# Linear attention beside a small mixture block: the order of the first loads, and two zero products fewer

## The chip, the cores and the metric

The kernel runs on one core of one Trainium2 chip. Five engines work beside each other, each with its own list of instructions: TensorE (PE: matrix products and transposes, with its weight loads listed as PEld), VectorE (DVE), ScalarE (ACT), GpSimd (POOL) and SyncE (SP, which here only issues DMA transfers). ACT and POOL issue some transfers too. PE reads SBUF and writes PSUM, and what it writes must be copied from PSUM to SBUF by another engine before PE can use it again. The metric is the time of one execution in microseconds (us). Times within an execution are counted from the start of its span.

## What is computed

The input x has 2048 tokens of 640 features. All of what follows starts from the layer normalisation xn of x:

```python
xn = _layernorm(x, axis=-1)
return x + A(xn, wqkv, wo) + B(xn, w_r, w_gate, w_up, w_down)
```

Part A is linear attention with 32 heads of 20 features. From q, k, v = xn @ wqkv it forms phi(q) and phi(k), where phi(t) is t+1 for positive t and exp(t) otherwise, with 1e-6 added. It then takes kv = phi(k)^T v and z = the sum of phi(k) over the tokens for each head, and o = phi(q) kv / (phi(q) z), followed by a product with wo.

Part B scores every token by r = xn @ w_r and takes the 8 tokens of highest score. Those go through a gated block (silu(x w_gate) * (x w_up)) w_down, scaled by sigmoid(r), and the result is added to the rows of these tokens. Part B also passes xn itself on, so the output is x + xn + A + the eight rows.

## The kernel before

The tokens are cut into 16 tiles of 128 (t = 0 to 15), the features into 5 chunks of 128 (`KC`). The instructions of each engine stand in the order in which the program text issues them; nothing reorders them. An engine therefore waits at the first instruction whose inputs are not there, and everything behind it on that engine waits too.

**First loads (L108 to L118).** Two queues carry them. SP issues one half of x tile 0, x tiles 1 and 2, chunks 3 and 4 of the k weights (`wk`), chunks 0 and 1 of the q weights (`wq`), x tile 3, and x tiles 4 to 7 in one transfer. ACT issues the other half of x tile 0, chunks 0 to 2 of `wk`, and chunks 2 to 4 of `wq`. The column 640 of `wk` is not loaded with it: it takes the score weights w_r, which come by a small transfer on POOL, are transposed on PE into `prep` (L312), and are copied in by ACT (L313).

**Zero products (`warm_mm`, L273).** PE multiplies a tile of zeros, in products of 512 or 128 columns, whose results nobody reads. Eight long ones come first (L296), then the eight small products of the head mask (`mask_mm`), two more long ones (L298) and two of 128 columns (L305).

**Normalisation.** For each tile, DVE makes two statistics of 320 features (`ln_half`, L165), joins them (`ln_aggr`), and POOL raises the variance to the power one half (L178). For the first four tiles DVE then takes the reciprocal and writes xn (`ln_norm`, L193). Tile 0's xn is written in two pieces, of 256 and of 384 features.

**Transposes.** Tiles 0, 1 and 2 are transposed on PE (`tr_tile`, L202) and copied to `xnT` (`tr_evict`, L208): both copies of tile 0 and the first of tile 1 by ACT, the second of tile 1 by DVE, tile 2's by ACT. From tile 3 on a DMA transpose does it.

**The start of the products.** `k_mm(0)` takes 5 products of 512 columns, one for each chunk, then the transposes of tile 1 stand on PE, then 5 products of 129 columns. `k_mm(1)` and `q_mm(0)` follow, then the transposes of tile 2, then `ga_mm(0)`, which multiplies xn of tile 0 by phi(k) of tile 0 (`pk`). `pk` is made by two ACT passes over k (`ek`, `rk`, L215 and L218) and one DVE pass (L227).

**The loop (L438).** For each t from 2 to 15: k products, `ga_mm` of the tile before, q products on PE, and around them the statistics and normalisation of a tile two or three ahead, phi(k), phi(q), and the later loads. After the loop come the other Gram products, the choice of the 8 tokens, the gated block, the head-wise products and the output products.

Of the kernel before, what the change touches and what calls it, by code (L numbers as in the profile page):

```python
# [8 lines left out]
P = 128  # L9
S = 2048  # L10
D = 640
# [4 lines left out]
KC = D // P  # L16
FC = F // P
C = 8
TBLK = 512
# [11 lines left out]
EPS_BF16 = 1.0013580322265625e-05  # L31
PE_TR = 3
LN_FAST = 4
WARM = 10
LAST = (0, 320, 512, 640)

BF16 = mybir.dt.bfloat16
# [10 lines left out]
def kernel(  # L48
# [13 lines left out]
    nc = tc.nc  # L62
# [4 lines left out]
    x_v = A_x[0].rearrange("(t p) d -> p t d", p=P)  # L67
    out_v = out[0].rearrange("(t p) d -> p t d", p=P)
    wqkv_v = A_wqkv.rearrange("(kc p) n -> p kc n", p=P)
# [6 lines left out]
    def sb(shape, dt, name, tag=None):  # L76
        return big.tile(shape, dt, tag=tag or name, name=name)

    def pair(tag, name):
        return psum.tile([P, 2 * TBLK], F32, tag=tag, name=name)  # L80

    def bank(tag, name):
        return psum.tile([P, TBLK], F32, tag=tag, name=name)

    x_sb = sb([P, T, D], BF16, "x_sb")
# [5 lines left out]
    wq = sb([P, KC, D], BF16, "wq")  # L91
# [16 lines left out]
    nc.gpsimd.dma_start(wrow[:], B_w_r.rearrange("(kc p) -> kc p", p=P))  # L108
    nc.sync.dma_start(x_sb[:, 0, 0:HW], x_v[:, 0, 0:HW])
    nc.scalar.dma_start(x_sb[:, 0, HW:D], x_v[:, 0, HW:D])  # L110
    for t in (1, 2):
        nc.sync.dma_start(x_sb[:, t, :], x_v[:, t, :])
    nc.scalar.dma_start(wk[:, 0:3, 0:D], wqkv_v[:, 0:3, D : 2 * D])
    nc.sync.dma_start(wk[:, 3:KC, 0:D], wqkv_v[:, 3:KC, D : 2 * D])
    nc.scalar.dma_start(wq[:, 2:KC, :], wqkv_v[:, 2:KC, 0:D])
    nc.sync.dma_start(wq[:, 0:2, :], wqkv_v[:, 0:2, 0:D])
    nc.sync.dma_start(x_sb[:, 3, :], x_v[:, 3, :])
    nc.sync.dma_start(x_sb[:, 4:8, :], x_v[:, 4:8, :])  # L118


# [41 lines left out]
    def ln_half(t, h):  # L162
        if h == 0:
            stat[t] = work.tile([P, 2, nc.vector.BN_STATS_DIM], F32, tag="stats", name=f"st{t}")
        nc.vector.bn_stats(out=stat[t][:, h, :], in_=x_sb[:, t, h * HW : (h + 1) * HW])  # L165

    def ln_aggr(t):
        mv = work.tile([P, 2], BF16, tag="mv", name=f"mv{t}", bufs=4)
        nc.vector.bn_aggr(out=mv[:], in_=stat[t][:])
        sc = work.tile([P, 2], F32, tag="sc", name=f"sc{t}", bufs=4)  # L170
        sq = work.tile([P, 2], BF16, tag="sq", name=f"sq{t}", bufs=4)
        scal[t] = sc, sq
        (nc.vector if t < LN_FAST else nc.gpsimd).tensor_scalar(  # L173
            out=sq[:, 0:1], in0=mv[:, 1:2], scalar1=EPS_BF16, scalar2=None, op0=ALU.add
        )
        if t < LN_FAST:
            nc.vector.tensor_copy(sc[:, 0:1], mv[:, 0:1])
        nc.gpsimd.tensor_tensor(out=sq[:, 1:2], in0=sq[:, 0:1], in1=half[:], op=ALU.pow)  # L178
        if t >= LN_FAST:
            nc.gpsimd.tensor_tensor(out=sc[:, 1:2], in0=sq[:, 1:2], in1=neg1[:], op=ALU.pow)  # L180
            nc.gpsimd.tensor_copy(sc[:, 0:1], mv[:, 0:1])  # L181
# [6 lines left out]
    def ln_norm(t):  # L188
        sc, sq = scal[t]
        if t < LN_FAST:  # L190
            nc.vector.reciprocal(sc[:, 1:2], sq[:, 1:2])
        for a, b in ((0, 2 * P), (2 * P, D)) if t == 0 else ((0, D),):
            nc.vector.tensor_scalar(  # L193
                out=xn[:, t, a:b], in0=x_sb[:, t, a:b], scalar1=sc[:, 0:1], scalar2=sc[:, 1:2],
                op0=ALU.subtract, op1=ALU.mult,
            )
        if t >= PE_TR:
            nc.sync.dma_start_transpose(xnT[:, :, t * P : (t + 1) * P], xn[:, t, :])
# [74 lines left out]
    def warm_mm(n, count):  # L273
        for _ in range(count):
            nc.tensor.matmul(
                warm[:, 0:n], lhsT=zero[:], rhs=zero[:, 0:1].to_broadcast([P, n]), start=True, stop=True
            )
# [4 lines left out]
    def mask_mm():  # L282
        ps = pair("A", "mask")
        hf = hd[:].rearrange("p h d -> p (h d)")
        for b in range(NW):
            e0, lo, hi = windows(b)
            for a, z in ((lo, min(hi, TBLK)), (max(lo, TBLK), hi)):
                if a < z:
                    nc.tensor.matmul(
                        ps[:, a:z], lhsT=hf[:, e0 : e0 + P], rhs=hf[:, a:z],  # L290
                        start=(a in (0, TBLK)), stop=True, skip_group_check=True,
                    )
        nc.scalar.copy(maskm[:], ps[:, 0:D])

    nc.scalar.copy(hd[:], ident[:, 0:H].unsqueeze(2).to_broadcast([P, H, DH]))
    warm_mm(TBLK, WARM - 2)  # L296
    mask_mm()
    warm_mm(TBLK, 2)  # L298

    ln_stats(0)  # L300
    ln_half(1, 0)
    ln_half(1, 1)
    ln_norm(0)
    ln_aggr(1)
    warm_mm(P, 2)  # L305
    tra, trb = bank("D1", "tr0a").bitcast(BF16), pair("C", "tr0b").bitcast(BF16)
    tr_tile(0, tra, 0, 2)
    tr_evict(0, tra, 0, 2, nc.scalar.copy)
# [2 lines left out]
    prep = bank("D0", "prep").bitcast(BF16)  # L311
    nc.tensor.transpose(prep[:, 0:KC], wrow[:], ident[0:KC, 0:KC])  # L312
    nc.scalar.copy(wk[:, :, D], prep[:, 0:KC])  # L313
    ln_half(2, 0)
    ln_norm(1)
    ln_half(2, 1)

    iof = sb([P, 32], F32, "iof")
# [445 lines left out]
    for fc in range(FC):  # L764
        j, b = fc // 3, fc % 3
# [59 lines left out]
    for t in range(NPRE, T):  # L825
# [6 lines left out]
        else:  # L832
            for i in range(3):
                a, b = LAST[i : i + 2]
# [39 lines left out]
```

## Time and profile before

| | |
|---|---|
| median of 3 runs | 111.44 us (111.42 to 112.5) |
| the profiled execution | 110.64 us |
| its span, first to last instruction | 108.9 us |
| PE busy | 102.8 us (94%) |
| DVE busy | 79.8 us (73%) |
| ACT busy | 66.4 us (61%) |
| POOL busy | 35.3 us (32%) |
| PE idle before the k products, released by the load of wk | 0.8 us |

A row of the instructions in order of time gives the start, the duration, the engine, the line, the operation, what it writes and reads, its shape and how many were merged; in brackets stands how long the engine had been idle before it and what ended that. A row of the chain gives a start, a duration and what the chain went through. A row of a stretch gives its bounds and length, then the busy time and count of PE, PEld, DVE, ACT and POOL, the granted clock, the share of the DMA engines and GB/s. A row of transfers gives what is loaded, who issued it, its size and the time from issue to landing. In the rows of queues, q1 carries what SP issues and q10 what ACT issues; the columns are packets, MB and share of time.

### The profile page before, as it was taken

The page shows a single profiled execution, that of the slowest core. Times are in us where ns is not written, and L with a number is a line of the kernel's source. Part 1 is how long each engine was busy: PE and PEld are TensorE (multiplying, and loading weights), DVE is VectorE, ACT ScalarE, POOL GpSimd, SP SyncE. Part 2 cuts the span into 40 slices and gives each one's busy share as a digit, 9 for nine tenths or more (in the row PEclk, how much of TensorE's full clock was granted, in tenths as well). Part 3 has the DMA queues.
Part 4 walks back from the last instruction along what each step waited for, and adds up shares of the span by engine and source line. Part 5 has one row for each costly group of instructions (what it writes and reads, how often), then busy time and mean ns, then how long its engine had stood idle before and what let it go on. Part 6 is the DMA issues. An engine that isn't in the chain of part 4 may idle for free.

```text
span 108.9 us, 2936 instructions
## 1 busy us (share of the span) xinstructions
PE 102.8 (94%) x1131; PEld 68.4 (63%) x1145; DVE 79.8 (73%) x200; ACT 66.4 (61%) x119; POOL 35.3 (32%) x81
## 2 busy tenths in 40 slices
PE   6978999999999999999999999999999999999980
PEld 2435877766777667776677654456996555555550
DVE  3885999979999899997999896723028615929670
ACT  4346887797777977779777855559128455555100
POOL 5422268688897757862000000120002300000000
PEclk9999999999999999999999999999999999999999
DMA  2999062759597999999899992594784797899993
GB/s 73 312 383 316 3 66 43 186 142 148 125 275 107 291 284 195 382 367 235 280 343 392 389 392 88 101 328 103 194 239 135 238 307 240 232 289 389 359 323 123
DMA packets 27406, 25.64 MB, mean 235 GB/s; under 512 B 10880, under 2 KB 25472, under 8 KB 27392
## 3 DMA queue, kind: packets, MB, share of 16 engines
q1 hardware_dynamic: 24976, 23.37, 74.5%
q10 hardware_dynamic: 2240, 2.04, 5.8%
q8 instruction: 9, 0.15, 0.5%
q0 software_dynamic: 176, 0.04, 0.5%
q14 instruction: 5, 0.04, 0.2%
HBM read 17.37 MB, written 5.94 MB: 214 GB/s over the span
## 4 chain that ended last, share of the span: by engine, by line
PE 87%; DMA 6%; DVE 1%; SPq 1%; issue 1%; DVEq 0%
PE q L252 21%; PE k L240 20%; PE o L796 14%; PE gbA L534 6%; PE gaC L263 6%; DMA wk<-in_A_wqkv_dram 6%; PE gbC L631 4%; PE gaD L263 3%; PE gu L644 1%; DVE o_all L804 1%; PE pkv L709 1%; PE M L744 1%; PE zp L504 1%; PE pden L612 1%; PE o13a L796 1%
## 5 line engine op out<-in xcount | busy, mean ns | idle before, releaser
L240 PE MATMUL k<-wk,xnT 128*128 128x129 bf16 (+1 forms) x152 | 24.6, 296 | 1.4 <-DMA wk<-in_A_wqkv_dram 0.8
L252 PEld LDWEIGHTS <-wq 128*128 128x128 bf16 x400 | 23.6, 98 | 3.6
L252 PE MATMUL q<-xnT,wq 128*128 128x128 bf16 x400 | 25.0, 219 | 0.0
L796 PEld LDWEIGHTS <-pqT 128*128 128x128 bf16 x165 | 12.7, 98 | 9.3 <-issue 0.3
L240 PEld LDWEIGHTS <-xnT 128*128 128x128 bf16 x160 | 12.4, 98 | 9.0 <-issue 1.1
L215 ACT ACTIVATE eq<-q 128x640 bf16<-128x640 f32 x16 | 11.2, 703 | 10.0 <-PE q L252 9.9
L796 PE MATMUL o<-M,pqT 128*128 128x128 bf16 (+1 forms) x108 | 15.7, 298 | 0.1
L165 DVE BATCH_NORM_STATS2 st<-x_sb 128x6 f32<-128x320 bf16 x32 | 14.1, 478 | 1.1 <-DMA x_sb<-in_A_x_dram 1.1
L227 DVE SCALAR_TENSOR_TENSOR pk<-ek,rk 128x640 bf16<-128x640 bf16 x16 | 13.2, 823 | 2.2 <-ACT rk L218 1.7
L178 POOL TENSOR_TENSOR sq<-sq,half 128x1 bf16<-128x1 bf16 x16 | 12.3, 772 | 7.2 <-DVE sq L173 4.1
L227 DVE SCALAR_TENSOR_TENSOR pqT<-eq,rq 128x640 bf16<-128x640 bf16 x16 | 13.1, 818 | 0.2 <-ACT rq L218 0.2
L215 ACT ACTIVATE ek<-k 128x640 bf16<-128x640 f32 x16 | 11.3, 704 | 1.7 <-DVE r_all L442 0.3
L218 ACT ACTIVATE rq<-q 128x640 bf16<-128x640 f32 x16 | 11.2, 700 | 0.0
L218 ACT ACTIVATE rk<-k 128x640 bf16<-128x640 f32 x16 | 11.2, 698 | 0.0
L820 ACT CAST o_all<-o 128x640 bf16<-128x640 f32 x9 | 6.2, 692 | 6.1 <-PE o L796 6.1
L180 POOL TENSOR_TENSOR sc<-sq,neg 128x1 f32<-128x1 bf16 x12 | 9.1, 757 | 0.9
L263 PE MATMUL gaC<-pk,xn 128*128 128x512 bf16 x31 | 9.3, 377 | 0.0
L684 DVE TENSOR_TENSOR pqT<-pqT,rb 128x2560 bf16<-128x2560 bf16 (+1 forms) x5 | 6.0, 1221 | 4.3 <-DMA rb<-rscr 4.3
L582 POOL COPY xsT<-xnT 128x5 bf16 x8 | 1.2, 215 | 20.5 <-DMA zrel<-zpart 20.5
L193 DVE TENSOR_SCALAR xn<-x_sb,sc 128x640 bf16<-128x640 bf16 (+2 forms) x17 | 6.9, 411 | 1.0 <-POOL sc L181 0.8
L534 PE MATMUL gbA<-pk,xn 128*128 128x512 bf16 x30 | 7.1, 380 | 0.2 <-issue 0.2
L388 DVE TENSOR_TENSOR x_sb<-x_sb,xn 128x640 bf16<-128x640 bf16 x16 | 7.2, 484 | 0.0
(155 smaller groups left out, 122.1 us busy)
## 6 DMA issues: line engine op xcount, KB each, us to landing
xcp<-x_sb SPq DMA_DIRECT2D x4, 640.0 KB, 7.0
x_sb<-in_A_x_dram SPq DMA_DIRECT2D x3, 640.0 KB, 4.6
x_sb<-xcp SPq DMA_DIRECT2D x3, 640.0 KB, 8.3
out_dram<-o_all SPq DMA_DIRECT2D x11, 160.0 KB, 4.9
wg<-in_B_w_gate_dram SPq DMA_DIRECT2D x2, 768.0 KB, 5.9
wu<-in_B_w_up_dram SPq DMA_DIRECT2D x2, 768.0 KB, 6.7
rb<-rscr SPq DMA_DIRECT2D x5, 256.0 KB, 4.5
rb<-rscr SPq DMA_DIRECT2D x8, 128.0 KB, 3.5
```

The lines of the kernel that those rows point to most:

```text
L165: nc.vector.bn_stats(out=stat[t][:, h, :], in_=x_sb[:, t, h * HW : (h + 1) * HW])
L178: nc.gpsimd.tensor_tensor(out=sq[:, 1:2], in0=sq[:, 0:1], in1=half[:], op=ALU.pow)
L180: nc.gpsimd.tensor_tensor(out=sc[:, 1:2], in0=sq[:, 1:2], in1=neg1[:], op=ALU.pow)
L215: nc.scalar.activation(e[:], ps[:, 0:D], AF.Exp)
L218: nc.scalar.activation(r[:], ps[:, 0:D], AF.Relu)
L227: nc.vector.scalar_tensor_tensor(out=dst, in0=ea, scalar=1.0, in1=ra, op0=ALU.min, op1=ALU.add)
L240: nc.tensor.matmul(ps[:, a:b], lhsT=xnT[:, kc, t * P : (t + 1) * P], rhs=wk[:, kc, a:b], start=(kc == 0), stop=(kc == KC - 1),)
L252: nc.tensor.matmul(ps[:, m * P : (m + 1) * P], lhsT=wq[:, kc, m * P : (m + 1) * P], rhs=xnT[:, kc, t * P : (t + 1) * P], start=(kc == 0 an ...
L263: nc.tensor.matmul(gaC[:, c * TBLK : (c + 1) * TBLK] if c < 2 else gaD[:], lhsT=xn[:, t, c * P : (c + 1) * P], rhs=pk[:, t, 0:TBLK], start ...
L388: nc.vector.tensor_tensor(out=x_sb[:, t, :], in0=x_sb[:, t, :], in1=xn[:, t, :], op=ALU.add)
L534: nc.tensor.matmul(gbA[:, (c - 3) * TBLK : (c - 2) * TBLK], lhsT=xn[:, t, c * P : (c + 1) * P], rhs=pk[:, t, 0:TBLK], start=(t == 0), stop ...
L796: nc.tensor.matmul(ps, lhsT=pqT[:, m, t * P : (t + 1) * P], rhs=M[:, m, a:b], start=(m == M_ORDER[0]), stop=(m == M_ORDER[-1]),)
```

## The change

Four things are edited. The second part of the k weights is issued on SP ahead of x tile 2. The q weights are all issued by SP, in chunks 0 to 2 and 3 to 4, behind x tile 2, and x tile 3 goes to ACT's queue in place of the q weights that were there. Of the zero products, the two long ones behind the mask are dropped, and in front of the first transposes stand five of 128 columns, not two. On DVE, the normalisation of tile 1 stands ahead of both statistics of tile 2, not between them.

```diff
-WARM = 10
+WARM = 8
...
-    for t in (1, 2):
-        nc.sync.dma_start(x_sb[:, t, :], x_v[:, t, :])
+    nc.sync.dma_start(x_sb[:, 1, :], x_v[:, 1, :])
     nc.scalar.dma_start(wk[:, 0:3, 0:D], wqkv_v[:, 0:3, D : 2 * D])
     nc.sync.dma_start(wk[:, 3:KC, 0:D], wqkv_v[:, 3:KC, D : 2 * D])
-    nc.scalar.dma_start(wq[:, 2:KC, :], wqkv_v[:, 2:KC, 0:D])
-    nc.sync.dma_start(wq[:, 0:2, :], wqkv_v[:, 0:2, 0:D])
-    nc.sync.dma_start(x_sb[:, 3, :], x_v[:, 3, :])
+    nc.sync.dma_start(x_sb[:, 2, :], x_v[:, 2, :])
+    nc.scalar.dma_start(x_sb[:, 3, :], x_v[:, 3, :])
+    for a, b in ((0, 3), (3, KC)):
+        nc.sync.dma_start(wq[:, a:b, :], wqkv_v[:, a:b, 0:D])
     nc.sync.dma_start(x_sb[:, 4:8, :], x_v[:, 4:8, :])
...
-    warm_mm(TBLK, WARM - 2)
+    warm_mm(TBLK, WARM)
     mask_mm()
-    warm_mm(TBLK, 2)
...
     ln_norm(0)
     ln_aggr(1)
-    warm_mm(P, 2)
+    warm_mm(P, 5)
...
+    ln_norm(1)
     ln_half(2, 0)
-    ln_norm(1)
     ln_half(2, 1)
```

## The prediction

> **What bounds the kernel now.** I read the page first, then the chain of work that ended last, then the instructions of the first 14 us in order of time, and last the busy time of chosen stretches. From the page, the span and the chain by engine and line:
>
> ```profile
> span 108.9 us, 2936 instructions
> PE 87%; DMA 6%; DVE 1%; SPq 1%; issue 1%; DVEq 0%
> PE q L252 21%; PE k L240 20%; PE o L796 14%; PE gbA L534 6%; PE gaC L263 6%; DMA wk<-in_A_wqkv_dram 6%; PE gbC L631 4%; PE gaD L263 3%; PE gu L644 1%; DVE o_all L804 1%; PE pkv L709 1%; PE M L744 1%; PE zp L504 1%; PE pden L612 1%; PE o13a L796 1%
> ```
>
> TensorE is the end of nearly everything; the one other item of size is the load of `wk`. The start of the chain, and the busy time of the main loop:
>
> ```profile
> 2.19 6.13 DMA wk<-in_A_wqkv_dram
> 8.37 0.59 PE k L240 x2
> ...
> 9.54 1.28 PE k L240 x8
> ...
> 11.10 1.43 PE q L252 x25
> ```
> ```profile
> 13.00:63.00 50.00, 49.60 (x556) 36.08 (x561) 46.20 (x99) 38.97 (x73) 28.00 (x59) 1.00 0.91 235
> ```
>
> The second half of `wk` is issued at 2.19 and lands at 2.19+6.13 = 8.32; the fourth product of k0 starts at 8.37. From 13 to 63 us PE is busy 49.60 of 50.00 (first number after the length). So whatever is gained or lost ahead of 13 us moves PE's loop whole; nothing in the loop has spare PE time to take it up, and its inputs are timed by the loop itself. The case is decided before 13 us.
>
> **The change part by part.** The rows of the first nine microseconds:
>
> ```profile
> 1.04 3.60 PE L275 MATMUL warm<-zero 128*128 128x512 bf16 x8 [1.04 <-DVE zero L122]
> 2.75 0.72 ACT L295 COPY hd<-ident 128x640 bf16<-128x640 bf16 x1 [0.68 <-POOL ident masks.py:199]
> 4.43 0.74 PE L289 MATMUL mask<-hd 128*128 128x96 bf16 x8
> 4.99 1.21 PE L275 MATMUL warm<-zero 128*128 128x512 bf16 x4
> 5.35 0.64 DVE L193 TENSOR_SCALAR xn<-x_sb,sc 128x256 bf16<-128x256 bf16 x2
> 6.03 0.28 PE L202 MATMUL tr0a<-ident,xn 128*128 128x128 bf16 x2
> 6.14 0.33 PE L202 MATMUL tr0b<-ident,xn 128*128 128x128 bf16 x3
> 6.34 0.37 ACT L208 COPY xnT<-tr0a 128x256 bf16<-128x256 bf16 x1 [0.44 <-PE tr0a L202]
> 6.38 0.55 POOL L178 TENSOR_TENSOR sq<-sq,half 128x1 bf16<-128x1 bf16 x1 [1.32 <-DVE sc L177]
> 6.61 0.48 ACT L208 COPY xnT<-tr0b 128x384 bf16<-128x384 bf16 x1
> 6.77 0.82 PE L240 MATMUL k<-wk,xnT 128*128 128x512 bf16 x3 [0.19 <-ACT xnT L208]
> 7.16 0.45 DVE L193 TENSOR_SCALAR xn<-x_sb,sc 128x640 bf16<-128x640 bf16 x1
> 8.80 0.27 PE L202 MATMUL tr1a<-ident,xn 128*128 128x128 bf16 x2
> ```
>
> *Zero products.* Eight long ones take 4.43-1.04 = 3.39, or 0.42 each. The second group (two long, two of 128 columns) reaches to 6.03, so a short one costs (1.04-0.85)/2 = 0.10. Two long ones go (-0.85), three short ones come (+0.30): PE is free at about 5.5. What is late next is xn of tile 0, written in two pieces from 5.35 to 5.99, the first ready near 5.7. The first two transposes can start at 5.75 in place of 6.03; the last three still wait for 5.99. ACT's copy of the first pair moves from 6.34 to about 6.14 (it has been free since 5.90, by the 0.44 in its row), the other copy ends near 6.9, not 7.09. k0 starts at 6.57, 0.2 earlier.
>
> *wk ahead.* In the rows of q, 25 products of 128 columns take 1.43, 0.057 each, so a product of 512 takes 0.22. The five of k0's first half run from 6.57; the third waits for the second copy (6.94); the fifth ends its turn near 7.67, if `wk` is there by 7.2. The transposes of tile 1 follow. They need xn of tile 1, ready at 7.16+0.45 = 7.61. They start at 7.67 in place of 8.80: **1.13 earlier** on PE.
>
> *Is the data there?* Bytes moved up to four times, and two transfers for the lag from the last byte to the landing:
>
> ```profile
> 0.00:6.16 6.16, 5.12 (x23) 2.36 (x24) 3.98 (x27) 2.70 (x3) 2.71 (x10) 1.00 0.68 212
> 0.00:6.58 6.58, 5.53 (x26) 2.59 (x26) 4.39 (x29) 2.94 (x4) 2.92 (x11) 1.00 0.71 224
> 0.00:8.72 8.72, 6.70 (x31) 3.06 (x32) 5.58 (x32) 3.63 (x6) 3.26 (x11) 1.00 0.80 263
> 0.00:10.90 10.90, 8.81 (x50) 4.37 (x52) 7.12 (x39) 5.34 (x10) 3.81 (x12) 1.00 0.82 271
> ...
> 4.24 0.37 SPq L118 DMA_DIRECT2D x_sb<-in_A_x_dram  x1
> ...
> x_sb<-in_A_x_dram SPq DMA_DIRECT2D x1, 640.0 KB, 7.1
> ```
>
> The last number is GB/s from the start: 1.31 MB by 6.16, 1.47 by 6.58, 2.29 by 8.72, 2.95 by 10.9. The last transfer (x tiles 4 to 7, all 2.95 MB with it) lands at 4.24+7.1 = 11.3, a lag of 0.4 to 0.6. The second half of wk now has at most 1680 KB (1.72 MB, moved by about 7.2) with or ahead of it and lands at 8.32, so a lag of up to 1.1. I use 0.4 to 1.1. In the new order, even if all that ACT issues goes first: wk whole is 1280 KB (1.31 MB), landing 6.6 to 7.3, wanted at 7.2; x tile 2 is 1440 KB (1.47 MB), landing 7.0 to 7.7, wanted at 7.5; wq whole is 2240 KB (2.29 MB), landing 9.1 to 9.8, wanted near 9.8; x tiles 4 to 7 stay at 11.3. All fit, with little to spare. SP issues seven loads before and after, ACT three, so no queue is longer; ACT's work behind them (2.75) waits for `ident` for 0.68, which covers a few hundredths; without that cover they would cost just these.
>
> *Normalisation of tile 1 ahead of tile 2's statistics.* One statistic takes 478 ns, two in a row 0.88 us:
>
> ```profile
> L165 DVE BATCH_NORM_STATS2 st<-x_sb 128x6 f32<-128x320 bf16 x32 | 14.1, 478 | 1.1 <-DMA x_sb<-in_A_x_dram 1.1
> 9.92 0.88 DVE L165 BATCH_NORM_STATS2 st<-x_sb 128x6 f32<-128x320 bf16 x2
> ```
>
> So neighbours on DVE overlap by 0.08. xn of tile 1 hung on POOL's power (6.38 to 6.93), not on DVE, so the swap gains nothing, and one statistic that filled that wait now comes later, 0.4 of DVE time. The pair runs from 7.53 to 8.41, and DVE is free for the copy of tile 1's last three transposes at 8.33. Without the swap a late tile 2 would hold up tile 1.
>
> *What is late next.* The rows from there to the first product that uses pk:
>
> ```profile
> 9.28 0.36 DVE L208 COPY xnT<-tr1b 128x384 bf16<-128x384 bf16 x1 [1.27 <-PE tr1b L202]
> 11.76 0.82 DVE L227 SCALAR_TENSOR_TENSOR pk<-ek,rk 128x640 bf16<-128x640 bf16 x1
> 12.64 0.59 PE L263 MATMUL gaC<-pk,xn 128*128 128x512 bf16 x2
> ...
> 9.28:12.58 3.30, 3.23 (x43) 2.51 (x42) 3.16 (x13) 2.93 (x8) 1.12 (x2) 1.00 0.41 138
> ```
>
> DVE's copy moves from 9.28 to 8.33: **0.95 earlier**, while PE could be 1.13 earlier. From the copy to the end of pk (12.58) DVE is busy 3.16 of 3.30, so pk comes 0.95 earlier too, and ga0, which starts right behind it at 12.64, can gain no more. PE then waits about 0.2 there. That is the sum: **0.95 off** (0.7 to 1.13: x tile 2 up to 0.2 late, or DVE's small gaps closing). After 13 us both engines are shifted alike.
>
> The profiled execution took 110.64 us, span 108.9 and 1.7 around it; the sum gives 109.7. The median of the runs shown is 111.44, 0.8 above the profiled one, and is what is forecast: 111.44-0.95 = **110.5**.
>
> **A place where the Trainium skill speaks against it.** By the rows, the products ran at 0.42 per 512 columns until the last zero products and at full rate in the second transposes (three in 0.33, one taking 0.22, so 0.055 apart): the rate doubled near 6.0, 5 us after PE began, although the page's granted clock reads 9 of 10 throughout. "TensorE: Matmul & The Clock Gate" of the Trainium skill, Part 1, says that the clock is raised only after a busy window of about 3.4 us that runs free of the kernel's start; the 5 us agree with that, and by it the moment is drawn anew in each run. Its Part 4 adds that transposes do not count as busy the same way, which no run here shows yet.
>
> **The rivals.**
>
> *The low rate lasts longer (slower).* The change takes 0.55 us of activity out just ahead of the turn and opens gaps on PE between 5.5 and 6.6. Before, the wait for wk hid any low rate until 8.37; now nothing does. For it: the new k0 stands where the rate turned. Against: PE is busy from 1.04 to 5.5 all the same, and the 0.78 us gap before 8.37 did not drop the rate (two products of 512 in 0.59). Price: at the low rate 0.83 ns a column against 0.44, so 0.47 us lost for each microsecond past 6.57; it eats the whole gain at 6.57+0.95/0.47 = 8.6. If the rate starts afresh after the first gap and takes its 5 us again, it turns near 10.7: 1.95 lost, +1.0 net, 111.6 on the profiled execution and 112.4 on the median. By that page's window of 3.4 us, one more of them would end near 9.4, an estimate that lies between the two.
>
> *The loads behind wk are late.* Each 0.1 by which x tile 2 lands past 7.5 takes 0.1 from DVE's chain; wq late beyond 10.0 does the same to q0 (PE has the 0.2 spare). With x tile 2 at 8.0 or wq at 10.5 the gain is 0.45: 111.0. For it: margins of nothing to 0.5. Against: the bounds above already put ACT's bytes first.
>
> *The change doesn't do what it says.* Rows of the stretch from 3.2 to 4.4 us:
>
> ```profile
> q10 hardware_dynamic: 267, 0.34, 84.0%
> q1 hardware_dynamic: 50, 0.05, 13.4%
> ```
>
> The queue with ACT's loads (q10) took six times what SP's moved. If x tile 3, now on it, and the first k weights hold SP back, wk's second half lands no sooner than 8.0, and 0.3 is left: 111.1. Against: there are only 1280 KB to move by then in any order.
>
> *More is gained.* If the 0.8 by which the median exceeds the profiled run is a longer wait for wk, it goes as well: 109.7.
>
> **How the numbers follow.** Forecast 0.55, late loads 0.15, low rate 0.13, not as it says 0.07, more gained 0.10. A per cent, 1.1 us, is about what a measurement of this kernel can tell from no change. The forecast lies just within it; by the scatter of the runs nearly half of its chance falls beyond, 0.26, and with the last rival 0.36 is faster. Slower is the low rate at its full price, 0.09, and 0.02 for scatter. The rest, 0.53, is the same. The range goes from a little below the sum on the profiled run (109.7) to between the two prices of the low rate (111.6 and 112.4): 109.6 to 111.9.
>
> **What would show it.** k0's five products without a wait, from about 6.6; tr1 near 7.7; DVE's copy of tr1b near 8.3; ga0 near 11.7; the loop's spacing unchanged. Wrong, if products of 512 start 0.42 apart after 6.6, if DVE's statistics of tile 2 wait for x, or if q0 waits for wq.

## The result, and the profile after

The changed kernel took 110.24 us in the median of 22 runs (109.39 to 111.43), the kernel before 111.26 in 22 runs beside it (110.42 to 112.5). The ratio is 0.990, with a 95% interval of 0.9871 to 0.9928: one per cent faster, clear of noise. The ratio leaves out executions more than 1.5% above the fastest of their kernel. The profiled execution took 109.81 us, against 110.64.

From the page after: the span, and the chain by engine and by line.

```profile
span 108.0 us, 2937 instructions
PE 84%; DVE 9%; DMA 2%; issue 1%; POOL 1%; DVEq 0%
PE q L252 19%; PE k L240 18%; PE o L795 14%; PE gbA L533 6%; PE gaC L263 6%; PE gbC L630 4%; PE gaD L263 3%; DVE st L165 3%; DMA x_sb<-in_A_x_dram 2%; PE gu L643 2%; DVE xn L193 1%; DVE o_all L803 1%; PE pkv L708 1%; PE M L743 1%; PE zp L503 1%
```

The load of `wk` has left the chain. In its place stand 9% of DVE and 2% of the load of x (the first half of tile 0, which lands at 3.0 us): from there to ga0, the first product that uses pk, the chain now runs through statistics, normalisation and pk on DVE, but for one pass on POOL. The instructions of that start, in order of time:

```profile
4.99 0.72 PE L275 MATMUL warm<-zero 128*128 128x128 bf16 x5
...
5.75 0.40 PE L202 MATMUL tr0a<-ident,xn 128*128 128x128 bf16 x2
...
6.61 1.25 PE L240 MATMUL k<-wk,xnT 128*128 128x512 bf16 x5
...
7.16 0.45 DVE L193 TENSOR_SCALAR xn<-x_sb,sc 128x640 bf16<-128x640 bf16 x1
7.21 0.18 ACT L312 COPY wk<-prep 128x5 bf16<-128x5 bf16 x1 [0.25 <-DMA wk<-in_A_wqkv_dram]
7.62 0.89 DVE L165 BATCH_NORM_STATS2 st<-x_sb 128x6 f32<-128x320 bf16 x2
...
7.70 0.28 PE L202 MATMUL tr1a<-ident,xn 128*128 128x128 bf16 x2
...
8.42 0.34 DVE L208 COPY xnT<-tr1b 128x384 bf16<-128x384 bf16 x1
...
9.87 1.56 PE L252 MATMUL q<-xnT,wq 128*128 128x128 bf16 x25
...
10.88 0.82 DVE L227 SCALAR_TENSOR_TENSOR pk<-ek,rk 128x640 bf16<-128x640 bf16 x1
...
11.26 0.44 PE L202 MATMUL tr<-ident,xn 128*128 128x128 bf16 x5
...
11.75 0.59 PE L263 MATMUL gaC<-pk,xn 128*128 128x512 bf16 x2
```

k0's five products run without a gap (1.25 us from 6.61). The second half of wk is in by 7.21, when ACT's copy into the same tile stops waiting. Tile 1's transposes start at 7.70 and not 8.80, DVE's copy at 8.42 and not 9.28, and ga0 at 11.75 and not 12.64, 0.89 earlier. The span is 0.9 shorter. From ga0 to the last addition of the output the two traces keep that distance (93.48 us in both, worked out further down).

### The profile page after: what moved, and what is told of

The parts are those of the page before. It is cut to its first block, busy times and chain, and to the rows that moved or that the text cites. A ratio compares the mean times of both kernels' runs of the same rounds, so it can differ in the third digit from the quotient of the medians.

```text
span 108.0 us, 2937 instructions
## 1 busy us (share of the span) xinstructions
PE 102.8 (95%) x1132; PEld 68.4 (63%) x1146; DVE 79.9 (74%) x200; ACT 66.4 (61%) x119; POOL 35.4 (33%) x81
## 4 chain that ended last, share of the span: by engine, by line
PE 84%; DVE 9%; DMA 2%; issue 1%; POOL 1%; DVEq 0%
PE q L252 19%; PE k L240 18%; PE o L795 14%; PE gbA L533 6%; PE gaC L263 6%; PE gbC L630 4%; PE gaD L263 3%; DVE st L165 3%; DMA x_sb<-in_A_x_dram 2%; PE gu L643 2%; DVE xn L193 1%; DVE o_all L803 1%; PE pkv L708 1%; PE M L743 1%; PE zp L503 1%
```

## The experiments

The start of ga0 is read from one trace of each kernel. It shows the parts better than the whole time does, but it holds for that one execution: with the same loads, x tile 2 landed 0.4 us later in e4 than in the changed kernel. A difference of a few tenths therefore needs rows that say where it comes from. Kernels are compared with the kernel before on the same chip.

| kernel | DVE copy of tile 1 | ga0 | ratio to before (95%) |
|---|---|---|---|
| before | 9.28 | 12.64 | |
| changed | 8.42 | 11.75 | 0.990 (0.987 to 0.993) |
| e1, loads in the old order | 9.33 | 12.69 | 0.999 (0.995 to 1.003) |
| e2, without the swap on DVE | 9.14 | 12.50 | 0.996 (0.992 to 1.000) |
| e3, old zero products | 8.53 | 11.89 | 0.984 (0.979 to 0.989) |
| e4, pk ahead of tile 3 | 8.79 | 11.82 | 1.003 (0.998 to 1.007) |
| e5, x tile 2 later | 9.57 | 12.90 | 1.003 (0.999 to 1.007) |
| e6, no zero products | 9.77 | 13.37 | 1.006 (1.001 to 1.011) |
| e7, q weights on ACT again | 9.06 | 12.50 | 0.999 (0.996 to 1.002) |
| e8, tile 1's copy on ACT | (ACT, 8.33) | 11.80 | 0.987 (0.983 to 0.991) |
| e9, and x tile 2 on ACT's queue | (ACT, 8.57) | 12.04 | 0.991 (0.987 to 0.995) |

### e1: the loads in their old order

```diff
-    nc.sync.dma_start(x_sb[:, 1, :], x_v[:, 1, :])
+    for t in (1, 2):
+        nc.sync.dma_start(x_sb[:, t, :], x_v[:, t, :])
...
-    nc.sync.dma_start(x_sb[:, 2, :], x_v[:, 2, :])
-    nc.scalar.dma_start(x_sb[:, 3, :], x_v[:, 3, :])
-    for a, b in ((0, 3), (3, KC)):
-        nc.sync.dma_start(wq[:, a:b, :], wqkv_v[:, a:b, 0:D])
+    nc.scalar.dma_start(wq[:, 2:KC, :], wqkv_v[:, 2:KC, 0:D])
+    nc.sync.dma_start(wq[:, 0:2, :], wqkv_v[:, 0:2, 0:D])
+    nc.sync.dma_start(x_sb[:, 3, :], x_v[:, 3, :])
```

> The changed kernel with the loads in their old order; the zero products and the normalisation order stay changed. If the gain comes from the k weights' arrival: the second half of wk lands at 8.3 again, the transposes of tile 1 start at 8.8, DVE's copy of them at 9.3, ga0 at 12.6, the time is that of before (ratio 0.998 to 1.002). If the fewer zero products or the swap carry part of it: ga0 0.2 or more ahead of 12.6.

In order of time, in e1:

```profile
6.62 1.04 PE L240 MATMUL k<-wk,xnT 128*128 128x512 bf16 x3
...
8.42 0.59 PE L240 MATMUL k<-wk,xnT 128*128 128x512 bf16 x2 [0.77 <-DMA wk<-in_A_wqkv_dram]
```

The wait for wk is back (0.77) and with it all of the time. k0 starts 0.15 earlier than before, and this earlier start is lost in the wait. The fewer zero products and the swap bring nothing while the loads are in the old order.

### e2: without the swap on DVE

```diff
-    ln_norm(1)
     ln_half(2, 0)
+    ln_norm(1)
     ln_half(2, 1)
```

> The changed kernel with tile 1's normalisation back between the two statistics of tile 2. If DVE's order decides, as the prediction has it (a late tile 2 would hold up tile 1): the first statistic of tile 2 waits for x until 7.6, xn of tile 1 is ready near 8.5 in place of 7.6, the transposes start near 8.55, the copy near 9.2, ga0 near 12.5, so 0.1 of the 0.9 us is left. If the swap is worth nothing by itself: ga0 at 11.75 to 11.85.

```profile
7.55 0.49 DVE L165 BATCH_NORM_STATS2 st<-x_sb 128x6 f32<-128x320 bf16 x1 [1.23 <-DMA x_sb<-in_A_x_dram]
8.14 0.45 DVE L193 TENSOR_SCALAR xn<-x_sb,sc 128x640 bf16<-128x640 bf16 x1
8.51 0.48 DVE L165 BATCH_NORM_STATS2 st<-x_sb 128x6 f32<-128x320 bf16 x1
8.65 0.28 PE L202 MATMUL tr1a<-ident,xn 128*128 128x128 bf16 x2 [0.85 <-DVE xn L193]
```

As expected, to within 0.1: DVE stands 1.23 us at a statistic whose x has not landed, with the finished scale of tile 1 behind it, and PE waits 0.85 for xn where before it waited for wk. ga0 gains 0.14 of the 0.89. The new order of loads is worth little without the swap, and the swap nothing without the new order (e1): the two are one change. The row also gives the landing of x tile 2: 7.55.

### e3: the old zero products

```diff
-WARM = 8
+WARM = 10
...
-    warm_mm(TBLK, WARM)
+    warm_mm(TBLK, WARM - 2)
     mask_mm()
+    warm_mm(TBLK, 2)
...
-    warm_mm(P, 5)
+    warm_mm(P, 2)
```

> The changed kernel with the old zero products. If DVE sets the end: k0 starts near 6.77 and not 6.61, the transposes of tile 1 near 7.85 and not 7.70, but DVE's copy stays within 0.1 of 8.42 and ga0 within 0.1 of 11.75: no difference in time. If PE sets the end: ga0 0.15 to 0.2 later.

In order of time, in e3, and its chain by engine:

```profile
6.24 0.53 PE L202 MATMUL tr0b<-ident,xn 128*128 128x128 bf16 x3
...
7.17 0.45 DVE L193 TENSOR_SCALAR xn<-x_sb,sc 128x640 bf16<-128x640 bf16 x1
...
7.53 0.88 DVE L165 BATCH_NORM_STATS2 st<-x_sb 128x6 f32<-128x320 bf16 x2
...
8.16 0.33 PE L202 MATMUL tr1b<-ident,xn 128*128 128x128 bf16 x3
...
8.53 0.36 DVE L208 COPY xnT<-tr1b 128x384 bf16<-128x384 bf16 x1
```
```profile
PE 94%; DVE 1%; issue 0%; DVEq 0%
```

k0 starts at 6.92, tile 1's transposes at 8.05, DVE's copy at 8.53 and ga0 at 11.89, 0.14 later than in the changed kernel: just over the 0.1 allowed, and for the rival's reason. In this trace PE is last: DVE is done with the statistics at 8.41 and has to wait for the transposes, which end at 8.49. PE was later than expected because its low rate lasted longer: three transposes of tile 0 took 0.53, and 0.33 in the kernel before, with the same zero products ahead of them. At the expected start (k0 at 6.77) the transposes would have been there before DVE was free. The time shows no loss: its ratio of 0.984, from five runs, reaches into the interval of the changed kernel. The fewer zero products carry no gain that these runs can show.

### e4: pk ahead of tile 3

```diff
     ln_aggr(2)
-    ln_stats(3)
+    ln_half(3, 0)
...
     phi_vec(pk[:, 0, :], ker, False)
+    ln_half(3, 1)
+    ln_aggr(3)
...
-    ln_norm(3)
-    ln_stats(4)
     ga_mm(0)
     phi_vec(pk[:, 1, :], ker, False)
+    ln_norm(3)
+    ln_stats(4)
```

> The changed kernel with half of the statistics of tile 3, their joining and tile 3's normalisation moved on DVE behind the pass that makes pk of tile 0. If DVE's run of work up to pk is what holds ga0: pk ends near 11.1, ga0 starts right behind the transposes of tile 2 at 11.5, 0.2 earlier than 11.75; 0.2 less than the changed kernel. Rival: xn of tile 3 comes near 13.1 in place of 12.3, its DMA transpose lands near 16.5, k of tile 3 wants it near 16.9; if it lands later, PE waits there and the 0.2 is given back.

This one missed. In its profiled execution the loads were late as well, so ga0 came at 11.82, behind PE's own transposes of tile 2; pk was ready before that (10.67+0.82 = 11.49). Then more was lost than the 0.2 could have brought. Whom PE waited for from 14 to 40 us, and what DVE waited for from 8 to 20:

```profile
PE gaC L263 <- DVE pk L227: 1.4, 2, 0.8
```
```profile
DVE sc L191 <- POOL sq L178: 0.7, 2, 0.4
DVE xn L193 <- POOL sc L181: 0.5, 1, 0.5
DVE st L165 <- DMA x_sb<-in_A_x_dram: 0.4, 1, 0.4
```

The rival named the wrong wait: not the transposes of tile 3 but pk of later tiles held PE, twice, 1.4 us in all. With tile 3 put off, DVE arrives at the reciprocals and at the normalisation before POOL has their inputs ready, and stands idle; shortly ahead of the first of PE's two waits, which ends at 19.46, DVE had stood 0.52 for POOL. From ga0 to the last addition this trace takes 2.4 us more than that of the changed kernel; where the rest of the 2.4 was lost is open.

### e5: x tile 2 behind the first q weights

```diff
-    nc.sync.dma_start(x_sb[:, 2, :], x_v[:, 2, :])
     nc.scalar.dma_start(x_sb[:, 3, :], x_v[:, 3, :])
-    for a, b in ((0, 3), (3, KC)):
-        nc.sync.dma_start(wq[:, a:b, :], wqkv_v[:, a:b, 0:D])
+    nc.sync.dma_start(wq[:, 0:3, :], wqkv_v[:, 0:3, 0:D])
+    nc.sync.dma_start(x_sb[:, 2, :], x_v[:, 2, :])
+    nc.sync.dma_start(wq[:, 3:KC, :], wqkv_v[:, 3:KC, 0:D])
```

> The changed kernel with x tile 2 behind the first 480 KB of the q weights on SP. At 360 GB/s it lands 1.3 us later, near 8.9. If DVE's chain from tile 2's statistics to pk sets the end, as the prediction says (each 0.1 past 7.5 costs 0.1): the copy on DVE moves from 8.4 to 9.7, ga0 from 11.75 to 13.0, the time is 1.3 over the changed kernel and 0.4 over before. If PE sets it: the products wait for the copy alone and ga0 comes later by 0.3 at most.

```profile
8.77 0.89 DVE L165 BATCH_NORM_STATS2 st<-x_sb 128x6 f32<-128x320 bf16 x2 [0.89 <-DMA x_sb<-in_A_x_dram]
9.57 0.34 DVE L208 COPY xnT<-tr1b 128x384 bf16<-128x384 bf16 x1
...
12.90 0.59 PE L263 MATMUL gaC<-pk,xn 128*128 128x512 bf16 x2 [0.25 <-DVE pk L227]
```

The statistics start 1.15 later than in the changed kernel (8.77 against 7.62), the copy 1.15 later, ga0 1.15 later, and PE waits there for pk. DVE's chain sets the end, one for one, although wk was early.

### e6: no zero products

```diff
-    warm_mm(TBLK, WARM)
     mask_mm()
...
-    warm_mm(P, 5)
```

> The changed kernel without its zero products (the mask's products stay). If the low rate costs what the prediction says, 0.47 us for each microsecond past 6.6: products of k0 start 0.43 apart, and with the rate turning near 9.6 PE loses 1.4, of which 0.25 is covered by its wait for pk: ga0 near 12.9, slower than before by 0.2. If the rate does not hang on the zero products, or DVE hides it: ga0 at 11.75 to 12.0.

```profile
6.88 2.31 PE L240 MATMUL k<-wk,xnT 128*128 128x512 bf16 x5
...
9.20 0.53 PE L202 MATMUL tr1b<-ident,xn 128*128 128x128 bf16 x3
```

k0's five products take 2.31 where they took 1.25. ga0 comes at 13.37, half a microsecond later than expected. PE's transposes of tile 2 are 1.83 later than in the changed kernel (13.09 against 11.26) where 1.4 was expected: xn of tile 0 was 0.27 later in this execution, and 0.54 was lost behind the start of tile 1's transposes, the last three of which still ran at the low rate (0.53, not 0.33). ga0 is 1.62 later; the 0.2 that PE had waited there was covered, as expected, and PE, not DVE, is now last (pk was ready at 13.06). The time is 0.6% above before. So the zero products matter for the rate of what follows them, and the rival of the prediction was right that this rate has a price.

### e7: the q weights on ACT's queue again

```diff
-    nc.scalar.dma_start(x_sb[:, 3, :], x_v[:, 3, :])
-    for a, b in ((0, 3), (3, KC)):
-        nc.sync.dma_start(wq[:, a:b, :], wqkv_v[:, a:b, 0:D])
+    nc.scalar.dma_start(wq[:, 2:KC, :], wqkv_v[:, 2:KC, 0:D])
+    nc.sync.dma_start(wq[:, 0:2, :], wqkv_v[:, 0:2, 0:D])
+    nc.sync.dma_start(x_sb[:, 3, :], x_v[:, 3, :])
```

> The changed kernel with chunks 2 to 4 of the q weights on ACT's queue again, ahead of x tile 3, which SP loads behind the rest of them; only the second half of wk stays ahead of x tile 2. If total bytes decide: ahead of wk's second half and x tile 2 there may then be 320 KB more, wk lands between 7.2 and 8.0, x tile 2 between 8.0 and 8.6, DVE's copy near 9.1, ga0 near 12.4: 0.2 of the 0.9 left. If moving wk ahead is enough by itself: ga0 at 11.75 to 11.9.

```profile
6.61 1.28 PE L240 MATMUL k<-wk,xnT 128*128 128x512 bf16 x5
...
8.26 0.89 DVE L165 BATCH_NORM_STATS2 st<-x_sb 128x6 f32<-128x320 bf16 x2 [0.54 <-DMA x_sb<-in_A_x_dram]
```

wk is in time (five products in 1.28), but now 480 KB of q weights, not 160 KB of x tile 3, are issued on ACT ahead of x tile 2. DVE stands 0.54 for x tile 2 until 8.26, and ga0 is at 12.50, as total bytes said. Moving wk ahead is not enough; the q weights have to stand behind x tile 2.

### e8 and e9: shortening DVE's chain

e8 gives the second copy of tile 1 to ACT; e9 also swaps the queues of x tiles 2 and 3.

```diff
-        tr_evict(1, tr1b, 2, KC, nc.vector.tensor_copy)
+        tr_evict(1, tr1b, 2, KC, nc.scalar.copy)
```

> The changed kernel with the copy of tile 1's last three transposes on ACT and not on DVE. If DVE's run of work up to pk is what holds ga0 once wk is early: DVE goes from tile 2's statistics straight to joining them, pk ends near 11.35 and not 11.70, and ga0 starts right behind the transposes of tile 2, at 11.5 to 11.6 in place of 11.75; 0.2 less than the changed kernel, which the times can hardly show. Rival: ACT, now with 0.5 us more, makes the first pass over k of tile 0 late, and pk with it: ga0 at 11.75 or later.

> As the run before, and x tile 2 goes to ACT's queue behind the first k weights, x tile 3 to SP's in its place. If transfers are served about in the order of their issue: x tile 2 lands near 7.0 and not 7.6, its statistics start at 7.53 with no wait for x, and ga0 is at 11.5 to 11.6 also in executions where the loads are late. If SP's queue with the second half of wk is served first, x tile 2 lands as before and ga0 is as in the run before.

The chain of e8, in order of time, and the wait for wk in e9:

```profile
8.06 0.75 ACT xnT L208 x2
8.81 0.61 ACT ek L215
9.43 0.59 ACT rk L218
10.02 0.07 ACT r_all L401
...
10.13 1.56 PE q L252 x25
```
```profile
7.56 0.59 PE L240 MATMUL k<-wk,xnT 128*128 128x512 bf16 x2 [0.24 <-DMA wk<-in_A_wqkv_dram]
```

pk ends at 11.51 now (10.69+0.82), 0.2 earlier, but ga0 is at 11.80, because q0 starts at 10.13 and not 9.87. q0 writes the PSUM tile that k0 used, so it waits for ACT's three passes over k0, and these now stand behind ACT's second copy. In the changed kernel the two are all but level: ACT's last pass ends at 9.82 (9.65+0.17), q0 starts at 9.87. The rival was right that ACT would be late, but the price came through PSUM and not through pk. e9 missed its 11.5 to 11.6 as well: x tile 2 brought no wait (its statistics start at 7.50), but wk's second half landed at 7.52, 0.4 later than in the changed kernel, and k0 waited 0.24 for it. Neither version beats the changed kernel by more than the intervals leave open.

## Why the prediction was right

**The sum.** It said 0.95 off, and the trace shows 0.89 at ga0 and 0.9 in the span; the medians differ by 1.02. The median of before in the comparison was 111.26 and not 111.44, which is most of the difference between 110.5 forecast and 110.24 measured. The prediction took one per cent for about the least that can be told from no change; with 22 runs of each kernel the interval was about 0.3 per cent to either side.

**Step by step.** First transposes 5.75 (measured 5.75), k0 6.57 (6.61), tile 1's transposes 7.67 (7.70), DVE's copy 8.33 (8.42), ga0 11.69 (11.75). Only DVE's copy is off by more than 0.06, and the reason is the prediction's own term for x tile 2. Its load in the changed kernel, and the time from issue to landing:

```profile
2.20 0.47 SPq L114 DMA_DIRECT2D x_sb<-in_A_x_dram  x1
...
DMA to landing us min/median/max: 5.4/5.4/5.4
```

It landed at 2.20+5.4 = 7.6, where 7.5 was wanted, and the statistics start there, at 7.62. Where it landed earlier (e3, 2.20+5.1 = 7.3), they start 0.09 ahead of the end of the pass over tile 1 (7.53 against 7.17+0.45 = 7.62), as the prediction had it.

**The loads.** The prediction put wk at 6.6 to 7.3 and x tile 2 at 7.0 to 7.7. They came at 7.1 (1.72+5.4) and at 7.6: the upper halves of the ranges, and there was luck in that. The top of the ranges, a lag of 1.1, came from a count that is wrong twice over. What was issued with or ahead of the second half of wk was not 1680 KB but 1760 KB (80, 160, 160 and 320 on SP, 80, 480 and 480 on ACT), 1.80 MB, moved by 7.4 in the kernel before:

```profile
0.00:7.40 7.40, 6.16 (x29) 2.87 (x30) 4.97 (x31) 3.45 (x5) 3.26 (x11) 1.00 0.75 243
```

That gives 0.9 and not 1.1, and since the bytes are counted at their most, it is a lag of at least that. By the same count the changed kernel's two loads had 1.0 (7.1 less 6.16, 7.6 less 6.58), above the corrected figure. With the same loads e4's statistics of tile 2 waited for x until 7.99, a lag of 1.4 (7.99 less 6.58): the rival of late loads happened there.

**DVE as the bound.** That ga0 can gain no more than DVE's copy was the step that turned 1.13 into 0.95. The wait of 0.2 on PE came too: where PE is last, ga0 follows the start of tile 2's transposes by 0.28 (e3: 11.61 and 11.89), in the changed kernel by 0.49 (11.26 and 11.75). e5 shows the bound one for one, e8 its limit: with pk 0.2 earlier, PE is last, held by ACT's passes.

**The swap.** "Gains nothing" was right by itself (e1). Behind the new loads it is worth 0.75 us (12.50 against 11.75); the prediction said that without it tile 2 would hold up tile 1, but gave no size.

**The low rate.** In the trace of the changed kernel this rival did not happen: the five products of k0 took 1.25. In e3 a little of it did. Its price was right: 1.06 more for five products at the low rate (e6), which is 0.41 ns a column against the 0.39 used (0.83 less 0.44). The moment of the turn differs between executions. In e9 the products of the mask, from 4.07, already ran at full rate (0.46, against 0.74 before), in e4 the first transposes did; e1's products after 6.62 did not yet (three in 1.04, against 0.82 before):

```profile
4.07 0.46 PE L289 MATMUL mask<-hd 128*128 128x96 bf16 x8
...
5.69 0.29 PE L202 MATMUL tr0a<-ident,xn 128*128 128x128 bf16 x2 [0.54 <-DVE xn L193]
```

The zero products and the mask are the same in these three kernels. "TensorE: Matmul & The Clock Gate" of the Trainium skill, Part 1, has the window run free of the kernel's start; these rows agree. Whether transposes count less than products (its Part 4) no run here tells. How often the turn comes behind 6.6 in the changed kernel is not known, with one trace of it; that it came ahead of k0 in that trace was in part luck.

**"More is gained" fell.** Its premise was that the scatter of the runs sits in the wait for wk. That wait is gone, and the runs scatter as before: 109.39 to 111.43, against 110.42 to 112.5. The traces show where some scatter sits. The last step of the chain in the changed kernel, and in e2, with e2's span:

```profile
105.03 0.20 DVEq L868
```
```profile
106.11 0.20 DVEq L868
```
```profile
span 109.7 us, 2951 instructions
```

From ga0 to the end of this step it is 93.48 us in the changed kernel (105.23-11.75), 93.48 before (106.12-12.64), and 93.81 in e2 (106.31-12.50). What is left of the span is 2.8 in the changed kernel, 2.8 before, 2.6 in e1 (108.9-106.32, the end of the same step there), 3.4 in e2 and 3.8 in e8 (109.1-105.28). So these traces differ by up to 1.2 us after the last addition, while the last stores land, and by 0.3 at most between ga0 and that addition. What delays the end was not tried, and whether it is what made the median of before exceed its profiled run is not shown.

## What to carry to other kernels

Order loads by when each is wanted, and then look at the instruction order of the engine that reads them: a load moved back stalls everything queued behind its first reader, so reader and load have to move together. When a wait goes, follow each engine to the point where they meet again; the gain is that of the slowest of them, here DVE's 0.89 and not PE's 1.1. Read a change of one per cent by the start of one instruction at which the chains meet, here ga0, where the whole time scatters by 2 us; and since a trace is one execution, read with it when the loads landed and which engine came last.

## What was not expected of the hardware

The end of the span scatters by more than the change is worth: 2.6 to 3.8 us pass between the last DVE addition and the end, with the same stores in each kernel. The turn of PE's rate scatters too: it came ahead of 4.1 us in e9 and only behind 6.6 in e1, though PE began alike. And a copy moved to an engine with room (ACT) delayed PE by 0.26 us through a PSUM tile that ACT reads and so releases (e8).
